# A convolution kernel's set-up: transform matrix built from odd and even parts, parameters loaded first and turned early

## The chip, the cores and the metric

The kernel runs on one core of one Trainium2 chip. The metric is the device time of one execution in microseconds (us), lower is better, as the median of several runs. One further execution is taken with the hardware profiler, and its rows are what the text reads. The engines are TensorE (PE in the rows; its weight loads are PEld), VectorE (DVE), ScalarE (ACT), GpSimd (POOL) and SyncE (SP, whose only work is to issue transfers; SPq, ACTq and POOLq are issues).

## The reference

```python
def reference(x, w, mean, var, g, b):     # x: 2 x 2048 x 1024, w: 3 x 1024 x 1024, all bf16
    K = 3
    P = K // 2
    S = x.shape[1]
    xp = jnp.pad(x, ((0, 0), (P, P), (0, 0)))
    y = sum(jnp.einsum('bsc,cd->bsd', xp[:, k:k + S, :], w[k]) for k in range(K))
    inv_std = 1.0 / jnp.sqrt(var + 1e-5)
    y = (y - mean) * (g * inv_std) + b
    return _silu(y)
```

A convolution along the sequence with three taps, then a batch norm with given statistics, then SiLU.

## The kernel before

**Scheme.** The convolution is done in blocks of 6 output positions from 8 transformed input positions (a Winograd scheme). The 2048 positions of a batch make `NTB` = 342 blocks. Input is read in windows of 21 blocks: 127 or 128 positions on the partitions and 1024 channels along the row. There are `NWIN` = 17 windows per batch, the last with 6 blocks.

**Transform.** `transform` (matmuls at line 216) multiplies a window's 128-channel slice by the matrix `Rm` (128 positions x 8 transformed positions x 21 blocks), which also turns channels onto the partitions. The results go from PSUM to `T_sb` as bf16, on ScalarE (line 230) or VectorE (line 232), whichever has the smaller planned load. In the first batch a window has 8 matmuls and 2 evacuations, one on each engine as a rule.

**Weights.** For each of the 8 chunks of 128 output channels (`dc`), `pair_weights` (lines 160 to 162) builds six combinations of the taps w0, w1, w2 on GpSimd into `uch`, from the raw taps (`wch`) and scaled copies; the first and last of the 8 products use raw taps. Chunk 0 is loaded tap by tap by `load_chunk` (line 88), later chunks in pairs (line 85).

**Products.** A `unit` (chunk, batch) runs 8 products of 8 matmuls each (line 241), in the order given there. VectorE combines them (line 272), ScalarE copies some out of PSUM (line 279) and applies SiLU with `beta` and `sk` (line 316). Then a transposing transfer and stores follow.

**Order.** The schedule is manual: each engine runs its instructions in the order of the program.

- Set-up: GpSimd clears the padding row of the first window `xw0` (line 98), makes the index table `val` (iota, line 101), and fills rows 0 and 7 of `Rm` by eight selects (line 128). VectorE clears `Rm`, makes `E` (line 104) and adds every nonzero coefficient of the inner six rows into `Rm` (line 116). Then GpSimd makes the identity `ident`.
- First batch: windows 0 to 16 are loaded and transformed. SyncE issues window 0 in two parts (lines 202, 203), window 1, taps w0 and w2 of chunk 0, window 2, tap w1, window 3 and so on. In window 1's step `load_params` puts the four parameter loads on GpSimd's queue. Chunk 0's weights follow on that queue. Before the last window `turn_params` transposes the parameters on TensorE (line 182) into a PSUM bank that the last window uses next, and VectorE copies them out as `prmT` (line 183). `make_params` then computes `rstd`, `sc`, `beta` and `sk` on GpSimd (lines 186 to 192), behind chunk 0's weights and ahead of chunk 1's, and two memsets clear the unused columns of `yT` (line 351).
- Second batch: the transform is cut into 51 groups of 3, 3 and 2 slices, in four PSUM banks, and the first unit's matmuls are interleaved: `want` says how many must have been issued after group `gi`.
- Then come the other units.

**Transfers.** The loads that SyncE and ScalarE issue take eight semaphores in turn; an issue waits until the load eight places before it has landed. GpSimd's loads have others.

Of the kernel before, what the change touches and what calls it, by code (L numbers as in the profile page):

```python
# [9 lines left out]
ALU = mybir.AluOpType  # L10
FP32 = mybir.dt.float32
BF16 = mybir.dt.bfloat16
# [4 lines left out]
BT = [  # L17
# [8 lines left out]
]  # L26
C1 = -2.0 / 9.0
# [3 lines left out]
NJ = 8  # L31
WT = 21
# [3 lines left out]
def kernel(  # L36
# [10 lines left out]
    nc = tc.nc  # L47
    B, S, C = x.shape
    D = w.shape[2]
    P = 128  # L50
    CT = C // P
    DC = D // P
    assert S % P == 0 and C % P == 0 and D % P == 0
    NTB = (S + M_OUT - 1) // M_OUT
    assert NTB <= 512
    NWIN = (NTB + WT - 1) // WT

    NB = (NTB + P - 1) // P
    NP = NB * P
    ctx.enter_context(tc.manual_schedule())  # L60

    consts = ctx.enter_context(tc.tile_pool(name="consts", bufs=1))
# [13 lines left out]
    def open_weights(dp):  # L76

        wch = pair_tile[dp] = wpool.tile([P, 3, CT, 2 * P], BF16, name="wch")
        for h in range(2):
            raw[2 * dp + h] = [wch[:, k, :, h * P:(h + 1) * P] for k in range(3)]  # L80
# [6 lines left out]
    def load_chunk(dc, k):  # L87
        nc.sync.dma_start(out=raw[dc][k], in_=w_all[:, k, :, dc * P:(dc + 1) * P])  # L88

    open_weights(0)  # L90

    dummy = consts.tile([P, 2], FP32, name="dummy")
    nc.vector.memset(dummy, 0.0)
    nc.scalar.activation(dummy[:, 1:2], dummy[:, 0:1], ACT.Silu)


    xw0 = consts.tile([P, C], BF16, name="xw0")
    nc.gpsimd.memset(xw0[0:1, :], 0.0)
    Rm = consts.tile([P, NJ, WT], BF16, name="Rm")
    val = consts.tile([P, NJ, WT], I32, name="val")  # L100
    nc.gpsimd.iota(val, pattern=[[-1, NJ], [-M_OUT, WT]], base=0, channel_multiplier=1)
    E = consts.tile([P, NJ, WT], FP32, name="E")
    nc.vector.memset(Rm, 0.0)
    nc.vector.tensor_single_scalar(E, val, 0.0, op=ALU.is_equal)
    for k in range(NJ):
        j = 1
        while j < 7:
            v = BT[j][k]
            if v == 0:
                j += 1  # L110
                continue
            j1 = j
            while j1 + 1 < 7 and BT[j1 + 1][k] == v:
                j1 += 1
            nj = j1 - j + 1
            nc.vector.scalar_tensor_tensor(  # L116
                out=Rm[:, j:j1 + 1, :],
                in0=E[:, k:k + 1, :].to_broadcast([P, nj, WT]) if nj > 1 else E[:, k:k + 1, :],
                scalar=float(v),
                in1=Rm[:, j:j1 + 1, :],  # L120
                op0=ALU.mult,
                op1=ALU.add,
            )
            j = j1 + 1
    for j in (0, 7):
        for k in range(NJ):
            if BT[j][k] != 0:
                nc.gpsimd.affine_select(
                    out=Rm[:, j, :],
                    in_=Rm[:, j, :],  # L130
# [6 lines left out]
    ident = consts.tile([P, P], BF16, name="ident")  # L137
    make_identity(nc, ident)
    yTs = [consts.tile([P, M_OUT, NP], BF16, name=f"yT{i}") for i in range(2)]

    def scale_weights(dc, taps=(2, 1, 0), on_gpsimd=False):
        for k in taps:
            f = 2.0 if k == 1 else 4.0
            dst = wx[dc, k] = wtmp.tile([P, CT, P], BF16, name=f"w{k}x")
            if on_gpsimd:
                nc.gpsimd.tensor_scalar(dst, raw[dc][k], f, 0.0, op0=ALU.mult, op1=ALU.add)
            else:
                nc.scalar.mul(dst, raw[dc][k], f)

    def open_chunk(dc):  # L150
        wts[dc] = upool.tile([P, 6, CT, P], BF16, name="uch")

    def pair_weights(dc, n):

        w0, w1, w2 = raw[dc]
        e = wtmp.tile([P, CT, P], FP32, name=("e1", "e2", "eh")[n])
        a = wx[dc, 0] if n == 2 else w0
        c = wx[dc, 2] if n == 1 else w2
        odd = wx[dc, 1] if n else w1
        nc.gpsimd.tensor_tensor(e, a, c, op=ALU.add)  # L160
        nc.gpsimd.tensor_tensor(wts[dc][:, 2 * n], e, odd, op=ALU.add)  # L161
        nc.gpsimd.tensor_tensor(wts[dc][:, 2 * n + 1], e, odd, op=ALU.subtract)  # L162
# [2 lines left out]
    load = {"act": 0.0, "dve": 1.0}  # L165
    EVAC = {"act": (0.17, 0.14), "dve": (0.12, 0.17)}

    prm = consts.tile([4 * DC, P], BF16, name="prm")
    prmT = consts.tile([P, 4, DC], FP32, name="prmT")
    sk = consts.tile([P, DC], FP32, name="sk")  # L170
    beta = consts.tile([P, DC], FP32, name="beta")
    mhalf = consts.tile([P, DC], FP32, name="mhalf")
    rstd = consts.tile([P, DC], FP32, name="rstd")
    sc = consts.tile([P, DC], FP32, name="sc")

    def load_params():
        for q, ap in enumerate((var, g, mean, b)):
            nc.gpsimd.dma_start(out=prm[q * DC:(q + 1) * DC, :], in_=ap.rearrange("(dc p) -> dc p", p=P))

    def turn_params(bk):  # L180
        pv = ps_all[:, bk * 512:bk * 512 + 2 * DC].bitcast(BF16)
        nc.tensor.transpose(pv, prm, ident[0:4 * DC, 0:4 * DC])
        nc.vector.tensor_copy(prmT.rearrange("p q d -> p (q d)"), pv)

    def make_params():
        nc.gpsimd.memset(mhalf, -0.5)
        nc.gpsimd.tensor_scalar(rstd, prmT[:, 0, :], 1e-5, 1.0, op0=ALU.add, op1=ALU.mult)
        nc.gpsimd.tensor_tensor(rstd, rstd, mhalf, op=ALU.pow)
        nc.gpsimd.tensor_tensor(sc, prmT[:, 1, :], rstd, op=ALU.mult)
        nc.gpsimd.tensor_tensor(beta, prmT[:, 2, :], sc, op=ALU.mult)  # L190
        nc.gpsimd.tensor_tensor(beta, prmT[:, 3, :], beta, op=ALU.subtract)
        nc.gpsimd.tensor_scalar(sk, sc, C1, 0.0, op0=ALU.mult, op1=ALU.add)

    epool = ctx.enter_context(tc.tile_pool(name="epool", bufs=1))

    def load_window(xpool, bi, wi):
        ntile = min(WT, NTB - WT * wi)
        t_lo = M_OUT * WT * wi - 1
        t_hi = min(t_lo + M_OUT * ntile + 1, S - 1)
        kk = t_hi - t_lo + 1  # L200
        if t_lo < 0:
            nc.sync.dma_start(out=xw0[1:113, :], in_=x[bi, 0:112, :])  # L202
            nc.sync.dma_start(out=xw0[113:kk, :], in_=x[bi, 112:t_hi + 1, :])  # L203
            return xw0, kk, ntile
        xw = xpool.tile([P, C], BF16, name="xw")
        nc.sync.dma_start(out=xw[0:kk, :], in_=x[bi, t_lo:t_hi + 1, :])  # L206
        return xw, kk, ntile
# [114 lines left out]
    def run(gen, n=None):  # L322
        while n is None or n > 0:
            if next(gen, run) is run:
                return
            if n is not None:
                n -= 1
# [3 lines left out]
    with tc.tile_pool(name="xwin", bufs=10) as xpool:  # L331
        for wi in range(NWIN):
            window = load_window(xpool, 0, wi)
            if wi == 1:
                load_chunk(0, 0)
                load_chunk(0, 2)
                load_params()
            if wi == 2:
                load_chunk(0, 1)
            for h in range(2):  # L340
                transform(0, wi, window, 4 * h, 4, (2 * wi + h) % 4 * 2, 2)
            if wi == 5:
                open_chunk(0)
                for n, taps in ((0, ()), (1, (2, 1)), (2, (0,))):
                    scale_weights(0, taps, on_gpsimd=True)
                    pair_weights(0, n)
            if wi == NWIN - 2:
                turn_params((2 * wi + 2) % 4 * 2)
        make_params()
        for yT in yTs:  # L350
            nc.gpsimd.memset(yT[:, :, NTB:NP], 0.0)

        first = unit(0, 0, 0, NTB, (0, 1, 2, 3), yTs[0], late, seven_first=True)
        load["act"] = load["dve"] = 0.0
        gi, done = 0, 0
        for wi in range(NWIN):
            window = load_window(xpool, 1, wi)
            if wi == 6:
                for k in (0, 2, 1):
                    load_chunk(1, k)  # L360
            for ct0, n in ((0, 3), (3, 3), (6, 2)):
                transform(1, wi, window, ct0, n, 4 + gi % 4, 3)
                gi += 1
                want = 52 * gi // (3 * NWIN)
                run(first, want - done)
                done = want
        load_weights(1)
        run(first)
# [41 lines left out]
    for ui, (dc, bi) in enumerate(units[1:-1], 1):  # L410
        yT = yTs[ui % 2]
# [16 lines left out]
    dc, bi = units[-1]  # L428
    yT = yTs[(len(units) - 1) % 2]
# [66 lines left out]
```

## Time and profile before

| what | value |
|---|---|
| median of 3 runs | 198.79 us (196.91, 198.79, 200.22) |
| profiled execution | 199.23 us |
| its span (first to last instruction) | 197.4 us |
| TensorE busy | 177.2 us, 90% of the span |
| GpSimd busy | 171.6 us, 87% |
| VectorE busy | 149.3 us, 76% |
| ScalarE busy | 138.6 us, 70% |
| transfers | 32.31 MB, mean 164 GB/s |

Busy times are averages over stages with different limits. Most of the chain that ended last is TensorE (80% of the span, nearly all of it the products of line 241); 7% is transfers, most of that the last output; 4% is VectorE. The first batch's transform ends at about 23.5 us, the interleaved stage at about 41.8 us, and the units then run to about 177 us, with the last unit's combination and stores behind. In a group's row the columns are start, length, engine, line, operation, tiles and sizes, and the count; in brackets stands how long the engine sat idle before it and what ended that. All times in rows are from the span's start.

### The profile page before, as it was taken

How to read it: one execution, taken by the hardware profiler on the slowest of the kernel's cores; microseconds unless marked ns; L12 is line 12 of the kernel's file. 1: busy time of each engine (PE TensorE's matmuls, PEld its weight loads, DVE VectorE, ACT ScalarE, POOL GpSimd, SP SyncE). 2: the span in 40 equal slices, each digit the busy share in tenths (PEclk: the TensorE clock that was granted, in tenths of full speed). 3: DMA queues.
4: the chain of work that ended last, by engine and by line, in shares of the span. 5: the costliest groups of instructions: out<-in, count | busy, mean ns of one | idle time of the engine just before them, and what ended most of it. 6: DMA issues, size and time to landing. Idle time of an engine off the chain costs nothing.

```text
span 197.4 us, 3893 instructions
## 1 busy us (share of the span) xinstructions
PE 177.2 (90%) x1379; PEld 126.4 (64%) x1379; DVE 149.3 (76%) x344; ACT 138.6 (70%) x254; POOL 171.6 (87%) x115
## 2 busy tenths in 40 slices
PE   0789799989999999999999999999999999999700
PEld 0688588856666666666666666666666666688500
DVE  6369798995969696968778786969696969699910
ACT  3459678879489848966984898489848966585800
POOL 7899999999999999999999999999999999206060
PEclk9999999999999999999999999999999999999965
DMA  5999999910608397979384799848392929297672
GB/s 136 280 387 332 330 233 342 300 38 2 120 0 164 66 192 207 241 166 193 60 171 86 148 297 209 165 97 158 71 182 44 200 52 204 47 182 127 104 147 65
DMA packets 85433, 32.31 MB, mean 164 GB/s; under 512 B 71772, under 2 KB 80998, under 8 KB 85414
## 3 DMA queue, kind: packets, MB, share of 16 engines
q1 hardware_dynamic: 84767, 31.00, 70.1%
q0 software_dynamic: 608, 1.06, 2.8%
q8 instruction: 11, 0.18, 0.3%
q14 instruction: 8, 0.07, 0.1%
q10 hardware_dynamic: 39, 0.01, 0.0%
HBM read 14.82 MB, written 8.39 MB: 118 GB/s over the span
## 4 chain that ended last, share of the span: by engine, by line
PE 80%; DMA 7%; DVE 4%; SPq 2%; POOL 1%; ACT 1%; issue 1%; POOLq 0%; ACTq 0%
PE ps_all L241 73%; PE ps_all L216 7%; DMA o_sb<-yT 4%; DVE T_sb L232 4%; DMA xw<-in_x_dram 2%; POOL out_dram L395 1%; SPq L206 1%; SPq L88 1%; ACT T_sb L230 1%; POOLq L491 0%; DVE y L272 0%; POOL out_dram L399 0%; SPq L203 0%; SPq L202 0%; ACT m L279 0%
## 5 line engine op out<-in xcount | busy, mean ns | idle before, releaser
L241 PE MATMUL ps_all<-T_sb,uch 128*128 128x342 bf16 (+2 forms) x816 | 123.9, 299 | 1.6 <-ACT m L279 1.6
L241 PEld LDWEIGHTS <-uch 128*128 128x128 bf16 x816 | 76.8, 97 | 34.3 <-issue 1.1
L316 ACT ACTIVATE yT<-y,beta,sk 128x342 bf16<-128x342 f32 (+2 forms) x102 | 64.6, 653 | 24.1 <-DVE y L272 24.1
L272 DVE SCALAR_TENSOR_TENSOR y<-ps_all,y 128x342 f32<-128x342 f32 (+2 forms) x102 | 45.4, 487 | 1.3
L241 PE MATMUL ps_all<-T_sb,wch 128*128 128x342 bf16 (+2 forms) x272 | 43.8, 300 | 0.1
L216 PE MATMUL ps_all<-Rm,xw 128*128 128x168 bf16 (+1 forms) x272 | 31.9, 254 | 8.0 <-DVE Rm L116 5.4
L230 ACT CAST T_sb<-ps_all 128x672 bf16<-128x672 f32 (+5 forms) x45 | 26.2, 606 | 12.2 <-PE ps_all L216 11.2
L216 PEld LDWEIGHTS <-xw 128*128 128x128 bf16 (+1 forms) x272 | 25.1, 106 | 13.5 <-POOL ident masks.py:199 5.4
L241 PEld LDWEIGHTS <-wch 128*128 128x128 bf16 x272 | 25.7, 97 | 11.6 <-DVE T_sb L232 0.3
L232 DVE CAST T_sb<-ps_all 128x672 bf16<-128x672 f32 (+3 forms) x40 | 26.3, 698 | 7.4 <-PE ps_all L216 7.2
L279 ACT COPY m<-ps_all 128x342 f32<-128x342 f32 (+2 forms) x51 | 21.8, 428 | 7.5 <-PE ps_all L241 5.4
L272 DVE SCALAR_TENSOR_TENSOR y<-ps_all,d 128x342 f32<-128x342 f32 (+2 forms) x51 | 22.0, 487 | 0.6
L272 DVE SCALAR_TENSOR_TENSOR y<-ps_all,s 128x342 f32<-128x342 f32 (+2 forms) x34 | 15.2, 489 | 9.1 <-ACT s L279 9.1
L272 DVE SCALAR_TENSOR_TENSOR d<-m,ps_all 128x342 f32<-128x342 f32 (+2 forms) x17 | 8.3, 490 | 16.8 <-ACT s L279 16.8
L395 POOL DMA_DIRECT2D out_dram<-o_sb x8 | 5.9, 866 | 14.8 <-DMA o_sb<-yT 14.8
L160 POOL TENSOR_TENSOR e<-wch 128x1024 f32<-128x1024 bf16 x8 | 17.0, 2128 | 0.9 <-DMA wch<-in_w_dram 0.9
L161 POOL TENSOR_TENSOR uch<-eh,w1x 128x1024 bf16<-128x1024 f32 x8 | 17.1, 2134 | 0.6
L161 POOL TENSOR_TENSOR uch<-e,wch 128x1024 bf16<-128x1024 f32 x8 | 17.1, 2133 | 0.6
L161 POOL TENSOR_TENSOR uch<-e,w1x 128x1024 bf16<-128x1024 f32 x8 | 17.0, 2131 | 0.6
L279 ACT COPY s<-ps_all 128x342 f32<-128x342 f32 (+2 forms) x34 | 14.6, 428 | 4.1 <-PE ps_all L241 0.4
L160 POOL TENSOR_TENSOR e<-wch,w2x 128x1024 f32<-128x1024 bf16 x8 | 17.0, 2130 | 0.1
L162 POOL TENSOR_TENSOR uch<-e,wch 128x1024 bf16<-128x1024 f32 x8 | 17.1, 2138 | 0.0
(46 smaller groups left out, 131.2 us busy)
## 6 DMA issues: line engine op xcount, KB each, us to landing
xw<-in_x_dram SPq DMA_DIRECT2D x30, 256.0 KB
out_dram<-o_sb SPq DMA_DIRECT2D x26, 192.0 KB
wch<-in_w_dram SPq DMA_DIRECT2D x9, 512.0 KB
out_dram<-o_sb SPq DMA_DIRECT2D x13, 120.0 KB
wch<-in_w_dram SPq DMA_DIRECT2D x6, 256.0 KB
out_dram<-o_sb POOLq DMA_DIRECT2D x4, 192.0 KB, 5.3
xw<-in_x_dram SPq DMA_DIRECT2D x2, 224.0 KB
o_sb<-yT SPq DMA_TRANSPOSE x15
```

The lines of the kernel that those rows point to most:

```text
L88: nc.sync.dma_start(out=raw[dc][k], in_=w_all[:, k, :, dc * P:(dc + 1) * P])
L160: nc.gpsimd.tensor_tensor(e, a, c, op=ALU.add)
L161: nc.gpsimd.tensor_tensor(wts[dc][:, 2 * n], e, odd, op=ALU.add)
L162: nc.gpsimd.tensor_tensor(wts[dc][:, 2 * n + 1], e, odd, op=ALU.subtract)
L216: nc.tensor.matmul(banks[:, at:at + NJ * ntile], lhsT=xw[0:kk, (ct0 + c) * P:(ct0 + c + 1) * P], rhs=Rm[0:kk, :, 0:ntile], start=True, sto ...
L230: nc.scalar.copy(dst, src)
L232: nc.vector.tensor_copy(dst, src)
L241: nc.tensor.matmul(ps_all[:, bk * 512:bk * 512 + c1 - c0], lhsT=lhsT, rhs=T_sb[bi][:, ct, j, c0:c1], start=start and ct == 0, stop=ct == C ...
L272: nc.vector.scalar_tensor_tensor(out=o, in0=i0, scalar=s, in1=i1, op0=ALU.mult, op1=op1)
L279: nc.scalar.copy(dst, src)
L316: nc.scalar.activation(yT[:, i, c0:c1], y[i], ACT.Silu, bias=beta[:, dc:dc + 1], scale=sk[:, dc:dc + 1])
L395: queue.dma_start(out=dst, in_=o_sb[a - n0:z - n0, :, nb])
```

## The change

- **Matrix.** The inner six rows of `Rm` form three pairs that differ only in the sign of the odd coefficients. Per pair, `parts` takes two operations (odd and even part side by side), and two more write even plus and even minus a multiple of odd: 12 operations in place of 25. Only rows 0 and 7 of `Rm` are cleared beforehand. The clear of `xw0`'s padding row moves from GpSimd to VectorE, behind the iota in the text, ahead of `E` on VectorE.
- **Parameter loads.** They are issued by ScalarE as its first instructions, ahead of its table load, instead of by GpSimd in window 1's step.
- **Turning.** `turn_params` runs behind window 1, into bank 2 (of window 0's second half), and issues the first two operations of `rstd` on GpSimd at once, ahead of chunk 0's weights. `make_params` keeps the other four operations, on VectorE. `mhalf` and the clears of `yT` move to the start of GpSimd's queue.
- **Tap w1** of chunk 0 is loaded in the step of window 3 instead of window 2, behind that window.
- **Pacing.** The first product matmul follows the second transform group of the second batch, not the first.

```diff
+    prm = consts.tile([4 * DC, P], BF16, name="prm")
+    for q, ap in enumerate((var, g, mean, b)):
+        nc.scalar.dma_start(out=prm[q * DC:(q + 1) * DC, :], in_=ap.rearrange("(dc p) -> dc p", p=P))
+
     dummy = consts.tile([P, 2], FP32, name="dummy")
     nc.vector.memset(dummy, 0.0)
     nc.scalar.activation(dummy[:, 1:2], dummy[:, 0:1], ACT.Silu)
 
-    xw0 = consts.tile([P, C], BF16, name="xw0")
-    nc.gpsimd.memset(xw0[0:1, :], 0.0)
     Rm = consts.tile([P, NJ, WT], BF16, name="Rm")
     val = consts.tile([P, NJ, WT], I32, name="val")
     nc.gpsimd.iota(val, pattern=[[-1, NJ], [-M_OUT, WT]], base=0, channel_multiplier=1)
+    xw0 = consts.tile([P, C], BF16, name="xw0")
     E = consts.tile([P, NJ, WT], FP32, name="E")
-    nc.vector.memset(Rm, 0.0)
+    parts = consts.tile([P, 3, 2, WT], FP32, name="parts")
+    nc.vector.memset(Rm[:, 0:NJ:NJ - 1, :], 0.0)
+    nc.vector.memset(xw0[0:1, :], 0.0)
     nc.vector.tensor_single_scalar(E, val, 0.0, op=ALU.is_equal)
-    for k in range(NJ):
...
-            nc.vector.scalar_tensor_tensor(
-                out=Rm[:, j:j1 + 1, :],
...
+    for n, odd in enumerate((1.0, 2.0, 0.5)):
+        row = BT[2 * n + 1]
+        assert [odd * row[k + 1] for k in (1, 3, 5)] == row[1:6:2] and row[6] == 1
+        rstt(parts[:, n], E[:, 1:3], row[2], E[:, 5:7])
+        rstt(parts[:, n], E[:, 3:5], row[4], parts[:, n])
+        rstt(Rm[:, 2 * n + 1], parts[:, n, 0], odd, parts[:, n, 1])
+        rstt(Rm[:, 2 * n + 2], parts[:, n, 0], -odd, parts[:, n, 1])
...
     yTs = [consts.tile([P, M_OUT, NP], BF16, name=f"yT{i}") for i in range(2)]
+    for yT in yTs:
+        nc.gpsimd.memset(yT[:, :, NTB:NP], 0.0)
...
-    def load_params():
-        for q, ap in enumerate((var, g, mean, b)):
-            nc.gpsimd.dma_start(out=prm[q * DC:(q + 1) * DC, :], in_=ap.rearrange("(dc p) -> dc p", p=P))
-
     def turn_params(bk):
         pv = ps_all[:, bk * 512:bk * 512 + 2 * DC].bitcast(BF16)
         nc.tensor.transpose(pv, prm, ident[0:4 * DC, 0:4 * DC])
         nc.vector.tensor_copy(prmT.rearrange("p q d -> p (q d)"), pv)
-
-    def make_params():
-        nc.gpsimd.memset(mhalf, -0.5)
         nc.gpsimd.tensor_scalar(rstd, prmT[:, 0, :], 1e-5, 1.0, op0=ALU.add, op1=ALU.mult)
         nc.gpsimd.tensor_tensor(rstd, rstd, mhalf, op=ALU.pow)
-        nc.gpsimd.tensor_tensor(sc, prmT[:, 1, :], rstd, op=ALU.mult)
-        nc.gpsimd.tensor_tensor(beta, prmT[:, 2, :], sc, op=ALU.mult)
-        nc.gpsimd.tensor_tensor(beta, prmT[:, 3, :], beta, op=ALU.subtract)
-        nc.gpsimd.tensor_scalar(sk, sc, C1, 0.0, op0=ALU.mult, op1=ALU.add)
+
+    def make_params():
+        nc.vector.tensor_tensor(sc, prmT[:, 1, :], rstd, op=ALU.mult)
+        nc.vector.tensor_tensor(beta, prmT[:, 2, :], sc, op=ALU.mult)
+        nc.vector.tensor_tensor(beta, prmT[:, 3, :], beta, op=ALU.subtract)
+        nc.vector.tensor_scalar(sk, sc, C1, 0.0, op0=ALU.mult, op1=ALU.add)
 
+    nc.gpsimd.memset(mhalf, -0.5)
...
             if wi == 1:
                 load_chunk(0, 0)
                 load_chunk(0, 2)
-                load_params()
-            if wi == 2:
+            if wi == 3:
                 load_chunk(0, 1)
...
-            if wi == NWIN - 2:
-                turn_params((2 * wi + 2) % 4 * 2)
+            if wi == 1:
+                turn_params(2)
         make_params()
-        for yT in yTs:
-            nc.gpsimd.memset(yT[:, :, NTB:NP], 0.0)
-
         first = unit(0, 0, 0, NTB, (0, 1, 2, 3), yTs[0], late, seven_first=True)
...
                 gi += 1
-                want = 52 * gi // (3 * NWIN)
+                want = 52 * max(gi - 1, 0) // (3 * NWIN - 1)
                 run(first, want - done)
```

More of the change, by code (lines that the diff above doesn't have):

```diff
@@ L101, with rstt @@
     nc.gpsimd.iota(val, pattern=[[-1, NJ], [-M_OUT, WT]], base=0, channel_multiplier=1)
+    xw0 = consts.tile([P, C], BF16, name="xw0")
     E = consts.tile([P, NJ, WT], FP32, name="E")
-    nc.vector.memset(Rm, 0.0)
+    parts = consts.tile([P, 3, 2, WT], FP32, name="parts")
+    nc.vector.memset(Rm[:, 0:NJ:NJ - 1, :], 0.0)
+    nc.vector.memset(xw0[0:1, :], 0.0)
     nc.vector.tensor_single_scalar(E, val, 0.0, op=ALU.is_equal)
-    for k in range(NJ):
[L106 to L116, printed above, removed]
-                out=Rm[:, j:j1 + 1, :],
[L118 to L124, printed above, removed]
+    def rstt(o, i0, f, i1):
+        nc.vector.scalar_tensor_tensor(out=o, in0=i0, scalar=float(f), in1=i1, op0=ALU.mult, op1=ALU.add)
+    for n, odd in enumerate((1.0, 2.0, 0.5)):
[5 more added lines that the diff above has]
+        rstt(Rm[:, 2 * n + 2], parts[:, n, 0], -odd, parts[:, n, 1])
     for j in (0, 7):
@@ L166 @@
     EVAC = {"act": (0.17, 0.14), "dve": (0.12, 0.17)}
-    prm = consts.tile([4 * DC, P], BF16, name="prm")
     prmT = consts.tile([P, 4, DC], FP32, name="prmT")
```

## Prediction

> **What bounds the kernel now.** I read the chain of work that ended last first, because it says which stage carries which microseconds. Its lines are start, length, work:
>
> ```profile
> 5.56 4.79 DMA xw<-in_x_dram
> 10.35 0.05 issue
> 10.39 4.11 PE ps_all L216 x28
> ...
> 16.31 6.23 DVE T_sb L232 x8
> 22.54 0.11 DVE prmT L183
> 22.64 0.04 issue
> 22.68 0.39 PE ps_all L216 x8
> 23.07 0.02 issue
> 23.10 0.37 DVE T_sb L232
> 23.46 0.05 issue
> 23.51 0.32 PE ps_all L241
> ...
> 41.80 135.53 PE ps_all L241 x942
> ```
>
> From 23.51 us on TensorE works nearly without a gap until 177 us, so whatever the change moves before 23.51 reaches the end unchanged, and nothing later is touched except small operations. Before 23.51 four things hold the chain one after another: the load of window 3 (to 10.35), TensorE (to 14.5), VectorE's evacuations (to 22.54), and a seam of 0.97 us from there to the first product (prmT, the last window's matmuls, its evacuation). The 25 operations that build the matrix are not in it. The timeline shows why:
>
> ```profile
> 2.35 2.91 DVE L116 SCALAR_TENSOR_TENSOR Rm<-E,Rm 128x21 bf16<-128x21 f32 x25
> ...
> 5.40 2.40 PE L216 MATMUL ps_all<-Rm,xw 128*128 128x168 bf16 x16 [5.40 <-DVE Rm L116]
> ...
> 8.32 1.30 PE L216 MATMUL ps_all<-Rm,xw 128*128 128x168 bf16 x8 [0.52 <-DMA xw<-in_x_dram]
> ```
>
> The matrix delays windows 0 and 1, but TensorE then waits for window 2's data anyway. In the trace's landing records windows 0 to 4 are complete at 3.66, 5.26, 8.27, 10.35 and 11.38, and the taps w0, w2, w1 of the first weight chunk at 6.41, 7.49 and 9.31. Last I read GpSimd, the busiest engine after TensorE:
>
> ```profile
> 30.71 1.67 POOL L188 TENSOR_TENSOR rstd<-rstd,mhalf 128x8 f32<-128x8 f32 x1
> ...
> 33.86 2.12 POOL L160 TENSOR_TENSOR e<-wch 128x1024 f32<-128x1024 bf16 x1
> ...
> 167.18 2.13 POOL L162 TENSOR_TENSOR uch<-eh,w1x 128x1024 bf16<-128x1024 f32 x1
> ```
>
> It runs unbroken from 7.63 to 169.3. Its last result is first read by the matmuls that start at 171.46, so it has about 2.1 us to spare there: it is close, but it does not bind.
>
> **Matrix.** Gone: 25 dependent operations (2.91 us) behind an E that started at 2.07. E waited for the iota at 1.73, which stood behind GpSimd's 0.94 us memset. Now iota can start near 0.8 and end at 1.1. VectorE clears Rm's two rows (below the 0.20 us of the whole clear) and xw0's row. The order listing gives that clear 512 elements; from the rows (2 elements 0.06, 168 elements 0.20) that is 0.06 to 0.94 us, and I take 0.5 by their slope. So E runs about 1.5 to 1.75. Of the 12 operations after it 7 wait for the one before (0.19 us apart in the old chain) and 5 don't (0.115): 1.3+0.6, ending near 3.7 (3.2 to 4.2). GpSimd's eight selects (2.10 us) end near 3.2, and window 0 has landed at 3.66. First matmul near 3.8 instead of 5.40: 1.6 us earlier. Worth: nothing. Windows 0 and 1 need 16 x 0.14 us, done by 6.4, and window 2 cannot start before about 8.2; the wait for it grows from 0.5 to 1.8 us.
>
> **Loads (C).** Two edits touch the data. Tap w1 is issued after window 3 instead of before it, so window 3 lands about 0.67 us (what windows 5 to 9 take each) after window 2: near 9.0. And the four parameter loads leave GpSimd's queue, where they were issued from 4.57 to 6.78 and landed from 8.5 to 10.84. While they landed, windows 3 and 4 took 1.04 and 1.03 us each; from window 5 on it was 0.66 to 0.69. For window 4 the order does not matter, since w1 is in front of it either way. Bounds: 11.38 as now, or 8.27+1.15 (a tap at w0's rate)+2x0.67 = 10.76 if the parameters were what slowed it. I take 10.76, the nearer to all the later rows. TensorE starts window 4 at 11.51 now (10.39 + 8 x 0.14), after the change at 10.76: gain 0.75. From there both kernels run alike, 1.12 us a window on TensorE and then 0.77 us a window on VectorE. The taps are not needed earlier: GpSimd wants w1 only after its first sum.
>
> That switch of pace is the unsure part. 168-column matmuls come every 0.14 us up to 14.5 us and every 0.072 us later, while the granted clock reads 1.00 in both stretches. After the change TensorE idles some 1.8 us before window 2 and 0.3 us before window 4, so the fast pace may start later than 14.5. Were it to come at 16, windows 7 and 8 would take 1.12 instead of 0.77 and C falls to 0.2; were it there at 11, VectorE alone would pace windows 4 to 15 and C becomes 2.2. I take 0.75 and keep both ends, with -0.4 below for the waits of the next part.
>
> The Trainium skill ("TensorE: Matmul & The Clock Gate", part 1, "What's actually happening") says that the array starts at half rate and is released only by a free-running window of about 3.4 us of sustained work. It speaks against this change: by an estimate from that page, steady work from 10.76 is released between 14.2 and 17.6, on average near 15.9, and C would be 0.2 instead of 0.75.
>
> **New waits.** On SyncE loads take eight semaphores in turn, each waiting for the load eight before it. With four parameter loads in front on ScalarE's queue, w2 waits for var, window 2 for g, window 3 for mean, w1 for b, and all of SyncE's queue stands behind. Landing: the 15-row load needed 2.4 us from issue (1.23 to 3.66), the old parameter loads 3.9 to 4.6. So var lands at 3.2 to 5.3 and b, issued some 1.5 us later, at 4.6 to 6.8. Today w2 is issued at 2.60 but its data come only when w0's are through, from about 5.2 on, and window 2's issue stands until 5.04. I take the low ends (same kind of queue): nothing lost. At the high ends the data stop for about 1 us, which gives the -0.4. ScalarE spends 4 x 0.45 us issuing, then 1.28 and 0.20: free near 4.1, or 4.9 at 0.67 each, against a first evacuation due at 4.6; window 2's wait hides 0.3.
>
> **Turning behind window 1 (A).** TensorE's transpose (0.18) waits for all four parameter loads and for the second evacuation; prmT (0.18 on VectorE) follows window 1's. Both lie in the wait for window 2. The seam loses them: window 16 finds its banks free about 0.8 us earlier, and after VectorE's last full evacuation only the short one (0.36, overlapped by 0.1) and the issue remain, 0.35 instead of 0.97: gain 0.62. GpSimd then has rstd (0.20) and pow (1.67) from about 7.0 to 9.0 ahead of its first weight sum, which started at 7.63: 1.3 later. In return 3.62 us (30.24 to 33.86) vanish, so GpSimd ends 2.3 earlier and TensorE about 1.6: the spare time stays above 2. VectorE gets four 128x8 operations behind the last evacuation, 0.12 to 0.2 each, 0.5 to 0.8 in all; it idled 0.70 there, and the group it evacuates next must be out only four groups (4 x 0.36 us) later. Were that cover gone, up to 0.8.
>
> **Pacing (B).** Two transform groups instead of one precede the first product: three more matmuls, 3 x 0.072 = 0.22, in the gap before 23.51 in which TensorE stood 0.44. The total of 52 interleaved products is unchanged. Gain 0.22.
>
> **Sum.** 0.62 + 0.22 + 0.75 = 1.6 us. The profiled execution took 199.23 (span 197.4): after, 197.6. It lies 0.44 above the median 198.79, so the median goes to 197.2.
>
> **Rivals.**
> First, the faster start pays in full: the steadier early work brings the fast pace before window 4, C = 2.2, gain about 3.0, time 195.8. For it: TensorE was busy just 3.7 of the 5 us before 10.4 and the new order has no wait between windows 2 and 3. Against: the 1.8 us hole.
> Second, the loads do not improve: window 4 still lands at 11.38, or the new waits hold SyncE. C between -0.4 and 0.1, only the seam is left: gain 0.4 to 0.9, time 198.1. The Trainium skill ("DMA: Bandwidth & Descriptors", "Issuing engines are not separate DMA queues") is on its side: moving loads to another issuing engine only saves the sequencer's time, so by that page C is 0.1 and the sum 0.9.
> Third, slower: the transpose sits in TensorE's in-order queue ahead of window 2 and needs the last of four small loads. Beyond 8.2 us a late b pushes window 2; 0.3 us are free (from 8.2 two windows of 1.12 end at 10.45, window 4 lands at 10.76), and the seam's 0.84 and today's window 4 start are used up when window 4 starts at 12.35, which is b landing near 10.1, 7.9 us after its issue against 4.6 at worst today. At 12 the time would be 200.7.
> That the edit does not act can be left out: the built instruction order shows all moves.
>
> **How the numbers follow.** Forecast 0.60 (gain 0.9 to 2.2, 196.6 to 197.9), first rival 0.17, second 0.15, third 0.05, unnamed 0.03. Single runs of this kernel spread over 3.3 us, so a median of a few carries about 1 us either way. The range takes the first rival less 0.8 and the second plus 1.2: 195.0 to 199.3. Two per cent (4.0 us) is about what a measurement of this kernel tells from no change; over that on the fast side needs the first rival and luck, 0.11; on the slow side most of the third, 0.04; the rest 0.85.
>
> **What would show it.** First matmul near 3.8, a wait of about 1.8 us before window 2 that names the xw load, window 3 near 9.0, window 4 near 10.8, the 0.14 to 0.072 switch at 14 to 16, no prmT between the last evacuations, first product near 21.9, GpSimd's last weight sum ending near 167. A first product at 23 proves the second rival, one below 21 the first, a wait of TensorE for prm the third.

## The result and the profile after

| what | before | after |
|---|---|---|
| median | 198.15 us (4 runs, 196.91 to 200.22) | 200.53 us (4 runs, 200.45 to 200.72) |
| ratio after / before | | 1.0105, 95% interval 1.0059 to 1.0151 |
| profiled execution, its span | 199.23, 197.4 us | 200.5, 198.7 us |
| first product | 23.51 us | 21.23 us |
| start of the long stretch of products behind the second transform | 41.80 us | 43.91 us |

The change makes the kernel about 1% slower; forecast was 197.2 us, with a range up to 199.3. (The medians of the kernel before that stand in this text, 198.79, 198.15, 199.1 and 198.84, are of different sets of its runs.) By the last two rows it is ahead by 2.28 us at the first product and behind by 2.11 us some 20 us later. So the loss lies between these two points and nowhere else. From there on both kernels run the same 942 matmuls in the same 135.53 us. Behind them the profiled executions differ by 0.8 us in the other direction (20.1 us of the span before, 19.3 after). Over all the profiles of this study this rest is 18.9 to 20.1 us with the same instructions in it, so I give it no cause.

First what went as predicted. TensorE's rows of the timeline after, the start of the first batch:

```profile
3.82 2.50 PE L210 MATMUL ps_all<-Rm,xw 128*128 128x168 bf16 x16 [3.82 <-DVE Rm L112]
...
8.04 4.17 PE L210 MATMUL ps_all<-Rm,xw 128*128 128x168 bf16 x29 [1.59 <-DMA xw<-in_x_dram]
```

The matrix is ready at 3.82 instead of 5.40, TensorE waits 1.59 us for window 2's data, and windows 2 and 3 follow each other without the old wait. The chain of waits after (start, length, work) shows both the gain and where it is lost:

```profile
5.76 4.79 DMA xw<-in_x_dram
10.60 1.26 PE ps_all L210 x8
...
14.71 5.45 DVE T_sb L226 x7
20.20 0.61 PE ps_all L210 x7
20.83 0.35 DVE T_sb L226
21.18 0.58 DVE sc L182
21.78 2.06 DVE beta L183
23.95 1.02 DVE sk L185
24.97 0.59 DVE T_sb L226
25.60 0.44 PE ps_all L210 x2
...
43.91 135.53 PE ps_all L235 x942
```

The seam has closed: the last window's short evacuation ends at 21.18, and the first product starts at 21.23. But the chain doesn't pass through that product. It goes on along VectorE, through three of the four small operations (`sc`, `beta`, `sk`), to an evacuation of the second batch that ends at 25.56. These three steps on 128x8 elements take 0.58, 2.06 and 1.02 us in the chain; the prediction had 0.12 to 0.2 each. The timeline of all engines over that stretch, with GpSimd's rows left in:

```profile
19.59 2.13 POOL L160 TENSOR_TENSOR uch<-e,w1x 128x1024 bf16<-128x1024 f32 x1
...
21.09 0.66 DVE L182 TENSOR_TENSOR sc<-prmT,rstd 128x8 f32<-128x8 f32 x1
...
21.68 2.12 POOL L161 TENSOR_TENSOR uch<-e,w1x 128x1024 bf16<-128x1024 f32 x1
...
21.78 2.05 DVE L183 TENSOR_TENSOR beta<-prmT,sc 128x8 f32<-128x8 f32 x1
...
23.86 0.17 DVE L184 TENSOR_TENSOR beta<-prmT,beta 128x8 f32<-128x8 f32 x1
23.89 1.05 POOL L145 TENSOR_SCALAR w0x<-wch 128x1024 bf16<-128x1024 bf16 x1
23.95 1.02 DVE L185 TENSOR_SCALAR sk<-sc 128x8 f32<-128x8 f32 x1
...
24.87 1.71 DVE L226 CAST T_sb<-ps_all 128x504 bf16<-128x504 f32 x3
...
25.60 0.44 PE L210 MATMUL ps_all<-Rm,xw 128*128 128x168 bf16 x2 [3.03 <-DVE T_sb L226]
```

Read the ends, start plus length. `sc` ends at 21.75 and GpSimd's sum at 21.72. The first `beta` ends at 23.83, GpSimd's next sum at 23.80. `sk` ends at 24.97, GpSimd's scaled tap at 24.94. Each long operation ends 0.03 us behind the one that was running on GpSimd when it started. The only short one, the second `beta` (0.17), starts at 23.86, in the gap between two GpSimd operations (23.80 to 23.89). All four have `prmT`, `rstd` or each other in SBUF on both sides; the evacuations, which read PSUM, run beside GpSimd at their old length. The table of waits does not show this: the time counts as VectorE's busy time.

From 21.09 to 24.97 VectorE does 3.88 us of what was costed at 0.5 to 0.8. Its evacuation, needed four groups later, comes late, and TensorE stands for 3.03 us (last row). The windows view of after (stretch, its length, then busy us and count for PE, PEld, DVE, ACT and POOL, the granted TensorE clock, the share of DMA engines, GB/s) shows a second loss:

```profile
22.60:25.60 3.00, 0.00 (x1) 0.00 (x0) 2.97 (x5) 0.44 (x1) 2.83 (x3) 0.95 1.03 197
25.60:28.70 3.10, 3.10 (x18) 2.52 (x18) 1.67 (x3) 1.07 (x2) 3.02 (x2) 0.50 0.97 273
28.70:34.00 5.30, 5.30 (x60) 4.53 (x58) 4.85 (x9) 4.22 (x8) 5.22 (x4) 1.00 0.98 330
```

After the stand TensorE is granted half its clock until about 28.7 us: 18 matmuls in 3.10 us, which at full clock are 1.55 us of work. The balance: -2.28 at the first product, -0.22 for the pacing, +3.03 for the stand, +1.55 for the half clock, together +2.08; measured between the two kernels at the stretch of products, +2.11.

### The profile page after: what moved, and what is told of

Same layout as the page of the kernel before. It is cut to its first block, busy times and chain, and to the rows that moved or that the text cites. A ratio compares the mean times of both kernels' runs of the same rounds, so it can differ in the third digit from the quotient of the medians.

```text
span 198.7 us, 3878 instructions
## 1 busy us (share of the span) xinstructions
PE 178.4 (90%) x1379; PEld 126.6 (64%) x1379; DVE 152.2 (77%) x336; ACT 138.4 (70%) x254; POOL 167.8 (84%) x106
## 4 chain that ended last, share of the span: by engine, by line
PE 78%; DMA 8%; DVE 6%; ACT 2%; POOL 1%; SPq 1%; issue 0%; POOLq 0%; ACTq 0%
PE ps_all L235 72%; PE ps_all L210 6%; DMA o_sb<-yT 4%; DMA xw<-in_x_dram 4%; DVE T_sb L226 4%; POOL out_dram L385 1%; ACT T_sb L224 1%; DVE beta L183 1%; SPq L200 1%; DVE sk L185 1%; DVE sc L182 0%; POOLq L481 0%; DVE y L266 0%; POOL out_dram L389 0%; SPq L88 0%
## 5 line engine op out<-in xcount | busy, mean ns | idle before, releaser
L235 PE MATMUL ps_all<-T_sb,wch 128*128 128x342 bf16 (+2 forms) x272 | 44.5, 302 | 0.2 <-DVE T_sb L226 0.2
L210 PE MATMUL ps_all<-Rm,xw 128*128 128x168 bf16 (+1 forms) x272 | 32.5, 253 | 8.8 <-DVE Rm L112 3.8
L235 PEld LDWEIGHTS <-wch 128*128 128x128 bf16 x272 | 25.9, 98 | 11.7 <-DVE T_sb L226 0.4
L385 POOL DMA_DIRECT2D out_dram<-o_sb x8 | 6.1, 892 | 14.3 <-DMA o_sb<-yT 14.3
L159 POOL TENSOR_TENSOR eh<-w0x,wch 128x1024 f32<-128x1024 bf16 x8 | 17.0, 2126 | 0.1
```

What stands on the lines that cost most here:

```text
L210: nc.tensor.matmul(banks[:, at:at + NJ * ntile], lhsT=xw[0:kk, (ct0 + c) * P:(ct0 + c + 1) * P], rhs=Rm[0:kk, :, 0:ntile], start=True, sto ...
L235: nc.tensor.matmul(ps_all[:, bk * 512:bk * 512 + c1 - c0], lhsT=lhsT, rhs=T_sb[bi][:, ct, j, c0:c1], start=start and ct == 0, stop=ct == C ...
L385: queue.dma_start(out=dst, in_=o_sb[a - n0:z - n0, :, nb])
```

## The experiments

The theory: a VectorE operation whose operands all lie in SBUF waits until the operation that GpSimd has running ends, and this wait alone turned the gain into a loss. The rivals: the four operations are slow by themselves (their form, their size, or the operations before them that they read from); another part of the change made the loss, the matrix or the early start; or the gain before the first product comes from elsewhere than the prediction said. The matrix, the seam with the pacing, the parameter loads and the tap are tried one at a time below. Rows give the 95% interval of the ratio to the kernel before, run on the same chip.

**The four operations back on GpSimd, all else as in the change.**

```diff
         nc.gpsimd.tensor_tensor(rstd, rstd, mhalf, op=ALU.pow)
-
-    def make_params():
-        nc.vector.tensor_tensor(sc, prmT[:, 1, :], rstd, op=ALU.mult)
...
+        nc.gpsimd.tensor_tensor(sc, prmT[:, 1, :], rstd, op=ALU.mult)
+        nc.gpsimd.tensor_tensor(beta, prmT[:, 2, :], sc, op=ALU.mult)
+        nc.gpsimd.tensor_tensor(beta, prmT[:, 3, :], beta, op=ALU.subtract)
+        nc.gpsimd.tensor_scalar(sk, sc, C1, 0.0, op0=ALU.mult, op1=ALU.add)
...
-        make_params()
```

> The changed kernel, with its four small operations (sc, two for beta, sk) on GpSimd directly behind the pow instead of on VectorE. Theory (on VectorE they waited for GpSimd's running operation: 3.9 us from 21.09 to 24.97, then TensorE stood 3.03 us and ran 3.4 us at half clock): here they take 4 x 0.2 us, first product near 21.2, no stall behind it, no half clock; the 3.03 + 1.5 us come back, 200.5 goes to about 196. Rival A (the pacing with two groups ahead, or the early start, makes the stall): it is still there and the time stays near 200.5.

Measured 197.39 us (8 runs, 196.51 to 197.88), ratio 0.9917 (0.9881 to 0.9954). GpSimd's rows of its timeline, then its chain:

```profile
8.99 0.21 POOL L180 TENSOR_TENSOR sc<-prmT,rstd 128x8 f32<-128x8 f32 x1
9.28 0.20 POOL L181 TENSOR_TENSOR beta<-prmT,sc 128x8 f32<-128x8 f32 x1
9.55 0.20 POOL L182 TENSOR_TENSOR beta<-prmT,beta 128x8 f32<-128x8 f32 x1
9.73 0.20 POOL L183 TENSOR_SCALAR sk<-sc 128x8 f32<-128x8 f32 x1
```

```profile
10.72 4.21 PE ps_all L208 x32
...
15.81 6.48 DVE T_sb L224 x9
22.33 0.32 PE ps_all L233
...
40.31 135.53 PE ps_all L233 x942
```

The same four operations on the same operands take 0.2 us each on GpSimd. The stand is gone, and so is the half clock, as the same two stretches of its windows view show:

```profile
22.40:25.60 3.20, 3.20 (x35) 2.73 (x36) 2.69 (x5) 2.28 (x6) 3.12 (x3) 1.00 1.05 216
25.60:28.70 3.10, 3.10 (x36) 2.67 (x35) 2.88 (x6) 2.63 (x6) 2.94 (x3) 1.00 0.93 256
```

Against the change, 36 matmuls instead of 18 in the second stretch. The products behind the transform start at 40.31 instead of 43.91, 3.6 us earlier, although the first product comes 1.1 us later here (22.33; the short matmul time set in at 14.3 us in this run and at 11.7 in the profile of the change). The median misses the expected 196 by 1.4 us; in the profile the later first product is the reason that 3.6 us come back and not some 4.6. This is the best version of the study, 0.8% below the kernel before, and the rest of the change is worth about what was forecast for all of it.

**A probe of forms.** The kernel before, with one more 128x8 VectorE operation behind each of units 1 to 14: seven forms, each twice, on constants, with results that nothing reads.

```diff
+    def probe(n):
+        free = ps_all[:, 3 * 512 + 400:3 * 512 + 408]
+        if n == 0:
+            nc.vector.tensor_tensor(po[:, 0:8], pa[:, 0:8], pb[:, 0:8], op=ALU.mult)
...
+        elif n == 5:
+            nc.vector.tensor_copy(free, pa[:, 0:8])
+            nc.vector.tensor_tensor(po[:, 0:8], pa[:, 0:8], free, op=ALU.mult)
...
         run(unit(dc, bi, 0, NTB, (half, half + 1, half + 2, half + 3), yT, late))
+        probe((ui - 1) % 7)
```

> The kernel before, with one extra 128x8 VectorE operation behind each of the units 1 to 14, on scratch tiles that nothing reads, in seven forms by turns while GpSimd builds weights: product of two SBUF tiles; tensor_scalar SBUF to SBUF; scalar_tensor_tensor of two SBUF tiles; tensor_scalar on 7 elements; copy SBUF to SBUF; product of an SBUF and a PSUM operand (with a copy into PSUM ahead of it); tensor_scalar from PSUM. Theory: the first two last until the running GpSimd operation ends (0.2 to 2.1 us, their ends on GpSimd's ends), those with a PSUM operand 0.17 to 0.25 us. Rival B (slow only where they stood, by code loading or a first use): all forms take about 0.2 us here. Open: the other forms.

One run, 200.0 us. VectorE's rows of its timeline, one of each form that tells something:

```profile
57.15 0.16 DVE L184 TENSOR_TENSOR po<-pa,pb 128x8 f32<-128x8 f32 x1
66.44 1.73 DVE L186 TENSOR_SCALAR po<-pa 128x8 f32<-128x8 f32 x1
...
103.77 0.16 DVE L195 TENSOR_TENSOR po<-pa,ps_all 128x8 f32<-128x8 f32 x1
112.86 0.15 DVE L197 TENSOR_SCALAR po<-ps_all 128x8 f32<-128x8 f32 x1
122.16 1.38 DVE L184 TENSOR_TENSOR po<-pa,pb 128x8 f32<-128x8 f32 x1
...
140.73 1.98 DVE L188 SCALAR_TENSOR_TENSOR po<-pa,pb 128x8 f32<-128x8 f32 x1
150.01 1.19 DVE L190 TENSOR_SCALAR po<-pa 128x7 f32<-128x7 f32 x1
```

One and the same instruction on the same constants takes 0.16 us at 57.15 and 1.38 us at 122.16. The first starts 0.08 us before a GpSimd operation ends at 57.23, and the next begins at 57.31; the second starts with 1.35 us of one still to run. All ten with every operand in SBUF, set beside the GpSimd operation that was running at their start:

| form | start, us | length | its end | GpSimd's end |
|---|---|---|---|---|
| two inputs | 57.15 | 0.16 | 57.31 | 57.23 |
| two inputs | 122.16 | 1.38 | 123.54 | 123.51 |
| one input and constants | 66.44 | 1.73 | 68.17 | 68.13 |
| one input and constants | 131.44 | 0.58 | 132.02 | 131.99 |
| two inputs and a constant | 75.72 | 0.91 | 76.63 | 76.60 |
| two inputs and a constant | 140.73 | 1.98 | 142.71 | 142.69 |
| one input, 7 elements | 85.01 | 0.23 | 85.24 | 85.20 |
| one input, 7 elements | 150.01 | 1.19 | 151.20 | 151.17 |
| copy | 94.29 | 1.50 | 95.79 | 95.76 |
| copy | 159.30 | 0.38 | 159.68 | 159.64 |

Nine of ten end 0.02 to 0.04 us behind GpSimd's operation, whatever the form; the tenth met a GpSimd operation that was all but over, and took its own 0.16. The copy into PSUM, the operation with one input in PSUM, and the one that reads PSUM alone took 0.15 to 0.16 us all six times, five of them within a GpSimd operation (the sixth, at 177.91, came after GpSimd's last sum). So neither the size nor the form makes it slow, nor what came before it (these read constants): it is where the operands lie and what GpSimd has running. The Trainium skill ("SBUF — State Buffer", "Who interferes with whom") states that VectorE and GpSimd share a port pair that one of them holds for a whole instruction, so that the other is blocked, not slowed; these ends agree with that. The same page names two inputs in SBUF, and copies and `tensor_scalar` in their fast modes, as what contends; the rows with 7 elements (0.23 and 1.19 us), a form that I had left open, end with GpSimd's operation too.

All these waits are for GpSimd operations of 1.0 to 2.1 us. Beside its selects of 0.2 to 0.3 us in the set-up before, the picture is mixed: one of VectorE's 25 matrix operations, all with their operands in SBUF, took 0.27 us (4.38 to 4.65) where those of its size took 0.17 to 0.19, and ends 0.03 us behind a select (4.33 to 4.62); another ran its 0.17 us (3.30 to 3.47) inside a select recorded from 3.28 to 3.54. For such short operations the wait is not shown as a rule.

**Only `sk` on VectorE**, the other three on GpSimd as in the best version.

```diff
+        nc.gpsimd.tensor_tensor(sc, prmT[:, 1, :], rstd, op=ALU.mult)
+        nc.gpsimd.tensor_tensor(beta, prmT[:, 2, :], sc, op=ALU.mult)
+        nc.gpsimd.tensor_tensor(beta, prmT[:, 3, :], beta, op=ALU.subtract)
 
     def make_params():
...
         nc.vector.tensor_scalar(sk, sc, C1, 0.0, op0=ALU.mult, op1=ALU.add)
```

> As the kernel with all four on GpSimd, but the last one (sk) stays on VectorE behind window 16's evacuation. Theory: it starts near 21.2 and ends when GpSimd's running operation ends, near 22.5 (GpSimd is 0.8 us later than in the changed kernel); the next evacuation starts there, TensorE stands some 0.7 us instead of 3.03, too short for the half clock; about 0.7 us slower than with four on GpSimd. Rival C (each such operation has a price of its own, 1.0 us for sk): ends at 22.2, no matter where GpSimd's operations end.

Measured 197.64 us (9 runs), ratio 0.9937 (0.9901 to 0.9974). From its timeline:

```profile
20.66 2.13 POOL L160 TENSOR_TENSOR uch<-e,w1x 128x1024 bf16<-128x1024 f32 x1
...
21.91 0.92 DVE L185 TENSOR_SCALAR sk<-sc 128x8 f32<-128x8 f32 x1
```

One operation alone still ends with GpSimd's (22.83 against 22.79). Its 0.92 us is near rival C's 1.0 as well, so it is the probe, with 0.16 to 1.98 us for the same few forms, that rules out a fixed price. TensorE loses only 0.24 us behind it (its next matmul starts at 23.46 instead of 23.22, 0.14 us after the one at 23.07), where 0.7 was expected, and there is no half clock. TensorE's one longer stand comes six us later:

```profile
29.48 0.39 PE L210 MATMUL ps_all<-Rm,xw 128*128 128x168 bf16 x3 [0.49 <-DVE T_sb L226]
```

The row names an evacuation, which ended at 29.46. But the weight load of this matmul waits for window 7 of the second batch, which landed at 29.43, so `sk` did not make this stand; the old matrix's run below shows the same wait. The medians are only 0.25 us apart from the best version, and the two intervals overlap, so what one such wait costs is not resolved in time. The price of the four is not four times that: three waits in a row (0.66, 2.05, 1.02) go far over the cover, and the half clock comes on top.

**The same operations at the same place on VectorE, without an operation that has all its operands in SBUF.** A copy of `rstd`, `sc` and the product lie in unused PSUM columns of bank 3; that is one operation more.

```diff
     def make_params():
...
+        f = [ps_all[:, 3 * 512 + 440 + 8 * i:3 * 512 + 448 + 8 * i] for i in range(3)]
+        nc.vector.tensor_copy(f[0], rstd)
+        nc.vector.tensor_tensor(f[1], prmT[:, 1, :], f[0], op=ALU.mult)
+        nc.vector.tensor_tensor(f[2], prmT[:, 2, :], f[1], op=ALU.mult)
+        nc.vector.tensor_tensor(beta, prmT[:, 3, :], f[2], op=ALU.subtract)
+        nc.vector.tensor_scalar(sk, f[1], C1, 0.0, op0=ALU.mult, op1=ALU.add)
```

> The changed kernel with the small operations still on VectorE at the same place, but rstd is first copied into unused columns of a PSUM bank and sc and the product for beta stay there, so that each of the five operations has at most one SBUF input and the two that read SBUF alone are gone (the copy writes PSUM). Theory (the price is the wait for GpSimd's running operation at the SBUF side, and the probe showed 0.15 to 0.16 us with a PSUM operand): five operations of 0.16 us, done about 1 us after window 16's evacuation, no 3 us stall, no half clock, about 197.4 as with the operations on GpSimd. Rival A (the place or the engine costs the time): still near 200.5.

Measured 197.84 us (12 runs, 197.11 to 198.89), ratio 0.9965 (0.9934 to 0.9995). From its timeline:

```profile
21.94 2.12 POOL L161 TENSOR_TENSOR uch<-e,w1x 128x1024 bf16<-128x1024 f32 x1
22.07 0.17 DVE L183 COPY ps_all<-rstd 128x8 f32<-128x8 f32 x1
...
22.69 0.16 DVE L186 TENSOR_TENSOR beta<-prmT,ps_all 128x8 f32<-128x8 f32 x1
22.77 0.16 DVE L187 TENSOR_SCALAR sk<-ps_all 128x8 f32<-128x8 f32 x1
...
22.98 0.32 PE L237 MATMUL ps_all<-T_sb,wch 128*128 128x342 bf16 x1 [1.18 <-DVE sk L187]
```

All five lie within one GpSimd operation (21.94 to 24.06) and take 0.16 to 0.17 us each, 0.86 us from the start of the first to the end of the last, against 3.88. The long stand and the half clock are gone. The 1.18 us in the last row are a price of the experiment: the scratch columns lie in the bank that the first product writes, so this product waits for `sk`. Even so it is 2.7 us below the change. With this the theory is shown: same engine, same place, the same work and one copy more, the same sums on GpSimd beside it, and what differs is the operands' place.

**The old matrix in the best version** (the 25 operations and GpSimd's clear of `xw0` put back).

```diff
-    nc.vector.memset(Rm[:, 0:NJ:NJ - 1, :], 0.0)
-    nc.vector.memset(xw0[0:1, :], 0.0)
+    nc.vector.memset(Rm, 0.0)
     nc.vector.tensor_single_scalar(E, val, 0.0, op=ALU.is_equal)
...
-        rstt(Rm[:, 2 * n + 1], parts[:, n, 0], odd, parts[:, n, 1])
-        rstt(Rm[:, 2 * n + 2], parts[:, n, 0], -odd, parts[:, n, 1])
+    for k in range(NJ):
...
```

> As the kernel with all four on GpSimd, but the matrix built as before (25 operations, xw0's row cleared by GpSimd). Step of the prediction: the matrix is worth nothing, since TensorE waits for window 2 anyway: first matmul near 5.4, window 2 near 8.1 as in the changed kernel, same time within 0.3 us. Rival D (the earlier start pays through an earlier full clock, which came at 11.66 us in the changed kernel and 14.49 before): clock later, 0.3 to 1 us slower.

Measured 197.44 us (8 runs), ratio 0.9931 (0.9887 to 0.9974), against 197.39 for the new matrix. Its first matmul is at 5.40 again, and window 2 starts at 8.28, when its data is there. The matrix is neither gain nor loss, as far as medians 0.05 us apart with intervals of some 0.8 us to either side can tell. Rival D's later clock did not come: the short matmul time set in at 10.1 us here.

This profile shows one thing more. Its first product is at 21.33, 1.0 us before the best version's, and still its long stretch of products starts at 40.80, 0.5 us behind. TensorE's row tells where the lead went:

```profile
29.35 0.39 PE L215 MATMUL ps_all<-Rm,xw 128*128 128x168 bf16 x3 [1.21 <-DMA xw<-in_x_dram]
```

It waits for window 7 of the second batch, the first load behind the three taps of chunk 1 in SyncE's queue: issued at 25.15, landed at 29.30. In the best version this load lands at 28.60, and TensorE gets to it at 28.86.

**The seam alone.** The kernel before with the turning moved to window 8 and the new pacing.

```diff
-            if wi == NWIN - 2:
+            if wi == 8:
                 turn_params((2 * wi + 2) % 4 * 2)
...
-                want = 52 * gi // (3 * NWIN)
+                want = 52 * max(gi - 1, 0) // (3 * NWIN - 1)
```

> The kernel before with the parameters turned behind window 8 instead of ahead of the last window, and the first product behind the second group: steps A and B of the prediction alone, the small operations as before on GpSimd. By the prediction 0.62 + 0.22 = 0.84 us faster than before, ratio 0.996; the seam from VectorE's last full evacuation to the first product 0.3 to 0.4 instead of 0.97 us. Rival: another evacuation or bank is late next and the seam keeps 0.9.

Measured 198.3 us (12 runs), before 198.84, ratio 0.9986 (0.9948 to 1.0024): 0.3 to 0.5 us for a forecast 0.84, not resolved from nothing. The seam does close (in its timeline the first product comes at 22.31, 0.32 us behind VectorE's last full evacuation, as in the change), but window 8 is no free place: TensorE stands 0.92 us for `prmT` there, and VectorE, which paces this stage, idles 0.83. So the gain of the seam alone stays open in time; that the turning costs nothing behind window 1 is seen only in the change and the versions made from it.

**The parameter loads alone.** The kernel before with the four loads first on ScalarE.

```diff
+    prm = consts.tile([4 * DC, P], BF16, name="prm")
+    for q, ap in enumerate((var, g, mean, b)):
+        nc.scalar.dma_start(out=prm[q * DC:(q + 1) * DC, :], in_=ap.rearrange("(dc p) -> dc p", p=P))
...
                 load_chunk(0, 2)
-                load_params()
```

> The kernel before with the four parameter loads issued first on ScalarE, all else as before. By the prediction the loads are what slowed windows 3 and 4: window 4 lands near 10.8 instead of 11.38, up to 0.75 us faster. Rival (moving the issue changes nothing for the transfers): 11.4, no difference.

Median 198.65 us (12 runs, 197.35 to 200.25 but for one of 475.16, which has no cause on record and is not in the ratio), ratio 1.0012 (0.9979 to 1.0046). TensorE's rows of its timeline:

```profile
8.40 1.30 PE L215 MATMUL ps_all<-Rm,xw 128*128 128x168 bf16 x8 [0.60 <-DMA xw<-in_x_dram]
10.59 2.70 PE L215 MATMUL ps_all<-Rm,xw 128*128 128x168 bf16 x18 [0.88 <-DMA xw<-in_x_dram]
```

Window 3 starts at 10.59, no earlier than before (10.39). Window 4 lands at 11.22 instead of 11.38, and TensorE, busy with window 3, gets to it only at 11.68. So taking the parameters off GpSimd's queue gains the kernel nothing.

**The tap alone.** The kernel before with w1 loaded behind window 3.

```diff
-            if wi == 2:
+            if wi == 3:
                 load_chunk(0, 1)
```

> The kernel before with tap w1 loaded behind window 3, all else as before. By the prediction window 3 lands near 9.3 instead of 10.35, but window 4 near 11.4 as before; TensorE waits there instead, so less than 0.2 us. Rival (an earlier window 3 is worth its 1 us): 1 us faster.

Measured 198.0 us (12 runs), ratio 0.9966 (0.9931 to 1.0001). TensorE's rows of its timeline:

```profile
8.24 2.42 PE L216 MATMUL ps_all<-Rm,xw 128*128 128x168 bf16 x16 [0.44 <-DMA xw<-in_x_dram]
10.82 2.42 PE L216 MATMUL ps_all<-Rm,xw 128*128 128x168 bf16 x16 [0.16 <-DMA xw<-in_x_dram]
```

Windows 2 and 3 run back to back, and window 4 starts at 10.82 instead of 11.51, with the parameters still on GpSimd's queue; its first product is at 23.10 instead of 23.51. I had expected next to nothing of it. The interval just reaches 1, so the time is not quite resolved, but the trace is clear: the move of the tap brings window 4 forward by 0.7 us, nearly all that the prediction gave to the loads together (0.75). Why it lands 0.6 us earlier (10.78 against 11.38) is open: in both kernels it is issued behind the same loads, which only change places. The landing records narrow it down. A load is complete with its sixteenth mark; before the change fourteen of window 4's marks are in by 10.66, and only the last two come at 11.22 and 11.38. With the tap moved all sixteen are in by 10.78, and with the parameter loads moved only the last is late (11.22). So the 0.6 us are two late parts of the load and not the whole of it; what holds them up is not shown.

## Why the prediction was wrong

**The failing step.** "VectorE gets four 128x8 operations behind the last evacuation, 0.12 to 0.2 each, 0.5 to 0.8 in all" and, for the lost cover, "up to 0.8". They took 0.66, 2.05, 0.17 and 1.02 us, 3.9 in all, because three of the four waited for GpSimd's running operation. The duration is that of VectorE's small operations in the set-up, before GpSimd's sums began. No row of before shows an all-SBUF operation of VectorE beside the 2.1 us sums: I took the nearest row by size and not by what lies beside it. A bound from the other side was there to read: GpSimd's 2.12 us rows, almost unbroken over the place where the four were to go. The rule of the page quoted with the probe spoke against the change, and the prediction did not weigh it. The cover was smaller than the four groups suggest: TensorE ran out of work at 22.57, the evacuation it then needed takes 0.63 us with its handover (24.97 to 25.60), so it had to start at 21.94, 0.85 us after the first small operation. 3.88 - 0.85 is the stand of 3.03, and the half clock made it 4.6 instead of "up to 0.8". None of the rivals named it; the slow one, a late parameter load, did not appear: no wait for `prm` stands among TensorE's.

**Turning (A)** was right: the gap from the last full evacuation to the first product was forecast at 0.35 instead of 0.97, and is 0.32 (20.91 to 21.23), a gain of 0.65 for a forecast 0.62.

**Pacing (B)** fits: the balance closes to 0.03 us with its 0.22. It was not measured by itself.

**Loads (C)** had the right effect, the wrong cause and a size that the run decides. Window 4 starts at 10.60 (forecast 10.76), 0.9 us earlier than before. The prediction gave that to the parameters and held that for window 4 "the order does not matter"; the runs of each alone give it, or 0.7 of it, to the order, that is to the tap. That the size still came out near the forecast is luck. The remaining 0.7 of C's measured 1.6 (2.28 less the seam's 0.65) come from the faster matmul pace, which set in at 11.66 us in this profile, between the forecast and the first rival (14 to 16, and 11). In nine other profiles of kernels with nearly the same start it set in between about 10 and 16 us, so this part belongs to the run and not to the change. The best version's profile, at 14.3, has its first product 1.18 us before the old one's (C and the seam were forecast at 1.37).

**The premise** that what the change moves before 23.51 "reaches the end unchanged" has a limit that it did not name: the load of the second batch's window 7, for which TensorE waited in the run with the old matrix. In the best version TensorE gets to that window 6.53 us after the first product (22.33 to 28.86). In the profile of the change the load landed at 28.36, and without the stand TensorE would by that estimate have been there at 27.76, so some 0.6 us of the 2.28 would have been lost anyway. The first rival, an earlier fast pace that pays in full, has the same limit.

**Second rival** (the loads do not improve): right for the parameters, wrong for the tap.

**The matrix** was worth nothing, with the wait for window 2 grown from 0.52 to 1.59 as forecast (1.8).

**GpSimd** had its 2 us to spare, as forecast, though its last sum ended at 171.37 and not near 167: it waited 4.2 us for ScalarE's scaled copy of tap w1 at one place. The product that reads the sum starts at 173.58.

Without the failing step the sum of 1.6 us fits what was measured: the best version, which is the change without it, is 1.7 us below the kernel before (199.1 to 197.39; by the interval 0.9 to 2.4). With C's cause wrong, that is in part luck.

## What to carry to other kernels

A small operation that moves to VectorE costs what GpSimd has running beside it if all its operands are in SBUF: here up to 2.05 us for 128x8 elements, and 0.16 with an operand in PSUM. Before moving it, read GpSimd's rows over the new place, not only VectorE's spare time; then put it where GpSimd is idle, keep an operand in PSUM, or leave it on GpSimd. Cost a lost cover from the moment when the next result is needed, and look whether the stand that follows is long enough to lower TensorE's clock (3.03 us was, 1.21 was not). And before counting a lead in full, look for the next load that will be wanted earlier with it.

## What the hardware showed that was not expected

- A VectorE operation that waits for GpSimd is recorded as busy, with nothing in the table of waits; it is found only by its length against its size, and by its end, 0.02 to 0.04 us behind GpSimd's in all 13 cases.
- After standing from 22.57 to 25.60 TensorE was granted half its clock up to about 28.7 us. The mean of 0.95 over the 3 us of the stand puts the drop 0.3 us before its end, after some 2.7 us. The stands of 0.49 us in the run with `sk` alone, of 1.18 in the one with PSUM and of 1.21 with the old matrix had no such result. The Trainium skill ("TensorE: Matmul & The Clock Gate", part 1) gives an idle window of about 3.4 us for the drop; here 3.03 us was enough, and the measurement decides.
- The change's four runs lie within 0.27 us, the four of before within 3.3. That fits a restart that GpSimd's row of operations sets, whenever the clock rose before it; but I have one trace of it, so this is argued and not shown.
